# Crossbar transfers of one batch change places: each expert pair's first 512 tokens ahead of its last 64

## The chip, the cores and the metric

The kernel runs on one core of a Trainium2 chip. The metric is the device time of one execution in microseconds (us). An execution under the profiler gives a trace, and the profile is read from it. The core's engines are TensorE (PE in the profile, with its weight loads apart as PEld), VectorE (DVE), ScalarE (ACT), GpSimd (POOL) and SyncE (SP). They run their own instruction streams in order and wait for each other by semaphores. SyncE computes nothing here: it issues transfers, one after the other, and 16 DMA engines carry them out. A transfer is done when it has landed, some time after its issue.

## The reference

Two layers run one after the other. The first is attention of 8 heads over keys and values that are averaged over groups of 8 tokens:

```python
k_p = k.reshape(B, H, Sp, pool, D).mean(axis=3)
v_p = v.reshape(B, H, Sp, pool, D).mean(axis=3)
scores = scale * np.matmul(q, k_p.transpose(0, 1, 3, 2))
...
return np.matmul(attn, v_p).astype(np.float32)
```

The second takes its output as x (8 batches, 576 tokens, width 512) and runs four attention experts of width 64. Each token keeps two of the four by a gate:

```python
for e in range(E):
    q = x @ wq[e]
    k = x @ wk[e]
    v = x @ wv[e]
    scores = scale * (q @ k.transpose(0, 2, 1))
    causal = np.triu(np.ones((S, S), dtype=bool), 1)
    ...
    ye = a @ v @ wo[e]
    for kk in range(K):
        mask = topk[:, :, kk] == e
        out += mask[..., None] * w[:, :, kk:kk + 1] * ye
```

## The kernel before

The 8 batches go through the same stages, several batches under way at once. The order of the work is written out by hand as one long string of tokens, SEQ (L622 to L693). A loop (L696 to L748) turns each token into instructions, and each engine runs its own in the order in which they stand there. A token has a name, arguments, a batch and, where it uses PSUM, a bank: "Y1:5@6" is Y with tile 1 for batch 5 in bank 6. Capitals are mostly matmuls, and the same small letter the step that reads their result. A "d" behind a token puts its copy on VectorE rather than ScalarE, a "p" leaves the write to the output for a later token (zs).

The 576 tokens of a batch are four tiles of 128 and a last one of 64. Two batches share their buffers, and their two last tiles of 64 lie side by side as one tile of 128 (tile 4). The four experts are handled as two pairs: pair 0 and pair 1.

The steps around the change are these:

- P and p compute a batch's expert queries and keys and copy them to SBUF (tile qk). V and v do this for the values (vaug), along with the gate's logits. Steps g0 to g9 compute the gate.
- S computes expert scores into two PSUM banks, s (L493, ScalarE) takes their exponential into etb, and a (L510, GpSimd) sets the masked half of the diagonal blocks to zero.
- B (Bv) multiplies etb with the values. Then bz (L545), bg (L547) and b (L552) divide by the sums of the exponentials, apply the gate and write osc, one buffer of 128 partitions per pair and batch parity. For batches 2 to 5 a batch's B is cut in two parts. In an odd batch part 0 holds the shared tile 4 and the first two full tiles, part 1 the last two full tiles. So the main transfer needs both parts, and the tail transfer needs part 0.
- osc has tokens in partitions, and the output product needs the pair's 2 x 64 channels there. For batches 0, 1, 6 and 7 TensorE transposes it (T, t). For batches 2 to 5 a crossbar transfer does it: F, the function crossbar (L574). It is issued from SyncE's queue and goes from osc to oT. F00 is pair 0's first 512 tokens (L580, here called main 0), F01 pair 0's last 64 (L577, tail 0); F10 and F11 are main 1 and tail 1.
- Y (L582) multiplies a tile's columns of oT with wop: one matmul for pair 0, then one for pair 1, summed in one PSUM bank. y (L592) copies the result to ofin, a ring of nine buffers, and z (L607) writes it to the output: 256 KB a tile. zs1:2 is the write of batch 2's tile 1. These writes are issued by SyncE too, in one stream with the crossbar transfers.

For batch 5 the string has F01, zs1:2, F00, F11, zs0:2 and F10 in this order on SyncE. F01 stands after b01:5 and b00:5 on VectorE, F11 after b10:5 and b11:5. The first readers of the mains are Y1:5 and Y3:5, which are followed on TensorE by S03:6, S10:7 and S11:7. The first reader of the two tails is Y4:5 (L687 of the string), since tile 4 holds the last 64 tokens of batches 4 and 5. The framework puts in the waits: a matmul that reads oT waits for the semaphore of the very transfer that wrote those columns, and a transfer waits for the osc that it reads.

```python
if tail:
    nc.sync.dma_start(out=oT[:, tcols(b)], in_=own[half(b), 4 * (1 - b % 2), :], transpose=True)
else:
    c = b % 2
    nc.sync.dma_start(out=oT[:, mcols(b)].rearrange("p (c n) -> p c n", n=128), in_=own[:, c : c + 4, :].rearrange("p c n -> p (c n)"), transpose=True)
```

Of the kernel before, what the change touches and what calls it, by code (L numbers as in the profile page):

```python
# [21 lines left out]
def kernel(  # L22
# [584 lines left out]
    def z(b, c, queue):  # L607
# [69 lines left out]
        a02:5 p_t0:6d g0:6 S11:5@4 F01:4 S00:6@6 s12:5 g2:6 V3:7@3 g3:6 g4:6 B01:5@2 s00:6 v3:7d F00:4 a12:5 Y2:3@0  # L677
        bz01:5 V4:7@3 bg01:5 s11:5 b01:5 V2:7@1 a00:6 y2:3dp Y0:3@2 v2:7 S10:5@6 a11:5 zs2:3 v4:7 y0:3dp S12:6@4
        S01:6@0 s10:5 B00:5@3 g5:6 zs0:3 g6:6 g7:6 P_t0:7@2 s12:6 g8:6 a10:5 g9:6 P_q0:7@6 p_t0:7d s01:6 bz00:5 a12:6
        bg00:5 Y1:2@2 b00:5 V1:7@7 p_q0:7d y1:2p F01:5 a01:6 S10:6@0 v1:7 S11:6@4 zs1:2 S02:6@2 s10:6 B10:5@6 g1:7  # L680
        F00:5 g2:7 Y0:2@7 s02:6 bz10:5 a10:6 B11:5@0 bg10:5 b10:5 P_k0:7@1 s11:6 bz11:5 a02:6 bg11:5 b11:5 F11:5
        B00:6@6 y0:2dp Y3:4@2 p_k0:7 a11:6 Y1:4@0 bz00:6 y3:4p zs0:2 bg00:6 F10:5 B11:6@1 b00:6 y1:4p S02:7@4 zs3:4
        bz11:6 S01:7@2 g0:7 bg11:6 S00:7@6 zs1:4 s02:7 b11:6 P_q1:7@0 g3:7 g4:7 g5:7 s00:7 g6:7 B10:6@1 a02:7 T00:6@4
        P_k1:7@5 bz10:6 bg10:6 p_q1:7 t00:6d a00:7 b10:6 s01:7 T11:6@4 Y1:5@6 p_k1:7d Y3:5@7 t11:6d y1:5p S03:6@0 a01:7
        S10:7@2 y3:5dp S11:7@4 s03:6 zs1:5 Y2:5@6 s10:7 g7:7 a03:6 zs3:5 g8:7 T10:6@7 Y0:5@0 t10:6d y2:5p B01:6@1 g9:7
# [90 lines left out]
```

## Time and profile before

| | before |
|---|---|
| median of 3 runs | 156.94 us (156.93 to 157.01) |
| profiled execution | 157.23 us, span 155.5 us |
| TensorE busy | 145.2 us, 93% of the span |
| ScalarE busy | 137.8 us, 89% |
| VectorE busy | 124.2 us, 80% |
| GpSimd busy | 89.0 us, 57% |
| granted TensorE clock, mean | 0.994 |

All times inside the profile are counted in us from the start of the span. Busy time of an engine is no proof that it is the bound. That is read from the chain of work that ended last, which is followed back from the last instruction to what released each step. In the views by tile and by line "x8" is the number of instructions. In the instructions in order of time the columns are start, length, engine (SPq is SyncE's queue of issues), line, operation, output, input and count; the brackets at the end give the idle time of that engine just before and what ended it. The length of an SPq row is the time that SyncE spent on issuing, not the time until the transfer landed.

### The profile page before, as it was taken

Reading aid. Unit: us, or ns where it says so; the run is one execution under the profiler, and the core shown is the slowest. Engines: PE = TensorE matmul, PEld = TensorE weight load, DVE = VectorE, ACT = ScalarE, POOL = GpSimd, SP = SyncE. Lnnn points to the kernel's source line nnn. Section 1 sums busy time; section 2 is a strip of 40 time slices with the busy share of each in tenths; the row PEclk is TensorE's granted clock in tenths of the full one; section 3 lists DMA queues with packets and bytes.
Section 4 is the critical chain, followed back from the end, with each engine's and each line's share of the span. In section 5 each row is a group of like instructions: output and inputs, shape, how many; then the busy total and the mean of one; then the engine's idle time right before and its main releaser. Section 6 shows DMA issues by size and latency. Waiting matters only on the chain.

```text
span 155.5 us, 5467 instructions
## 1 busy us (share of the span) xinstructions
PE 145.2 (93%) x2131; PEld 79.1 (51%) x2131; DVE 124.2 (80%) x407; ACT 137.8 (89%) x255; POOL 89.0 (57%) x160
## 2 busy tenths in 40 slices
PE   6998998999999999999999999999999999969980
PEld 2332452454664365455736556475465765526640
DVE  1862826889889889989898999999988888957860
ACT  3369579999999999999999999999999999969970
POOL 6996488999689988855999141224100434323200
PEclk9999999999999999999999999999999999999997
DMA  4999999999999999999999963431480552387894
GB/s 121 239 187 184 177 179 180 180 180 190 180 179 180 182 177 181 213 251 178 180 180 213 181 75 76 146 104 34 126 279 8 108 173 72 82 198 267 282 377 161
DMA packets 68746, 26.67 MB, mean 171 GB/s; under 512 B 62704, under 2 KB 63728, under 8 KB 68720
## 3 DMA queue, kind: packets, MB, share of 16 engines
q0 software_dynamic: 57264, 14.72, 95.0%
q1 hardware_dynamic: 11088, 10.88, 22.8%
q10 hardware_dynamic: 368, 0.72, 1.5%
q8 instruction: 16, 0.26, 0.7%
q14 instruction: 10, 0.08, 0.2%
HBM read 30.42 MB, written 9.44 MB: 256 GB/s over the span
## 4 chain that ended last, share of the span: by engine, by line
PE 54%; DMA 19%; POOL 9%; ACT 7%; DVE 4%; issue 4%; POOLq 0%; SPq 0%; DVEq 0%; ACTq 0%
PE psum L220 53%; DMA qraw<-in_q_dram 11%; DMA wst_q<-in_moe_wq_dram 5%; DMA oT<-osc 3%; POOL kraw L125 3%; POOL qraw L125 3%; ACT eta L330 3%; ACT etb L493 2%; POOL vraw L125 1%; POOL etb L510 1%; PE psum L229 1%; DVE qT L297 1%; ACT rza L353 1%; ACT rza L349 1%; DVE osc L552 1%
## 5 line engine op out<-in xcount | busy, mean ns | idle before, releaser
L493 ACT ACTIVATE etb<-psum 128x1024 bf16<-128x1024 f32 x48 | 47.2, 1029 | 0.7 <-PE psum L220 0.4
L510 POOL TENSOR_SCALAR_AFFINE_SELECT etb<-etb 128x256 bf16<-128x256 bf16 x64 | 25.9, 416 | 30.0 <-ACT etb L493 29.1
L330 ACT ACTIVATE eta<-psum 96x1024 bf16<-96x1024 f32 (+1 forms) x48 | 36.0, 807 | 0.6 <-PE psum L220 0.2
L220 PEld LDWEIGHTS <-etb 128*128 128x128 bf16 x480 | 18.6, 97 | 7.9 <-issue 2.8
L376 DVE TENSOR_TENSOR xT<-psum,rza 128x512 bf16<-128x512 f32 x32 | 20.5, 681 | 2.1 <-ACT rza L353 2.0
L220 PE MATMUL psum<-wop,oT 128*128 128x512 bf16 (+1 forms) x74 | 20.4, 373 | 1.7 <-DMA oT<-osc 1.4
L125 POOL DMA_DIRECT2D qraw<-in_q_dram x29 | 19.1, 661 | 4.3 <-DMA vraw<-in_v_dram 2.9
L220 PE MATMUL psum<-vaug,etb 128*128 128x65 bf16 x480 | 21.2, 193 | 0.2 <-POOL etb L510 0.2
L125 POOL DMA_DIRECT2D kraw<-in_k_dram x25 | 19.0, 765 | 3.0 <-issue 0.9
L125 POOL DMA_DIRECT2D vraw<-in_v_dram x24 | 18.5, 774 | 3.7 <-PE psum L220 2.9
L220 PE MATMUL psum<-wvg,xT 128*128 128x260 bf16 x144 | 20.5, 274 | 0.0
L220 PE MATMUL psum<-xT,wqp 128*128 128x64 bf16 (+1 forms) x128 | 19.6, 286 | 0.0
L220 PE MATMUL psum<-xT,wkp 128*128 128x512 bf16 (+1 forms) x128 | 19.5, 286 | 0.0
L552 DVE TENSOR_TENSOR osc<-psum,gt 128x256 bf16<-128x256 f32 (+2 forms) x40 | 16.6, 422 | 1.0
L220 PE MATMUL psum<-qk 64*128 64x64 bf16 (+4 forms) x192 | 16.1, 277 | 0.2
L220 PEld LDWEIGHTS <-xT 128*128 128x128 bf16 x144 | 12.7, 97 | 6.3 <-issue 2.5
L211 ACT COPY ofin<-psum 128x512 f32<-128x512 f32 (+1 forms) x25 | 13.9, 581 | 2.1 <-PE psum L220 1.8
L211 DVE CAST qk<-psum 128x512 bf16<-128x512 f32 (+1 forms) x24 | 14.6, 615 | 1.3 <-PE psum L220 0.6
L297 DVE STREAM_TRANSPOSE qT<-qraw 128x576 f32<-128x576 f32 (+1 forms) x17 | 13.2, 789 | 2.9 <-DMA qraw<-in_q_dram 2.2
L220 PE MATMUL psum<-qT,kpT 32*128 32x64 bf16 (+1 forms) x256 | 13.3, 289 | 1.6 <-ACT eta L330 0.6
L208 PE MATMUL psum<-warm 128*128 128x512 bf16 x41 | 12.8, 461 | 1.3 <-DVE onesd L176 1.3
L220 PE MATMUL psum<-eta,vp 96*32 96x512 bf16 (+1 forms) x256 | 13.1, 288 | 0.2 <-DVE vp L211 0.2
(78 smaller groups left out, 215.8 us busy)
## 6 DMA issues: line engine op xcount, KB each, us to landing
out_dram<-ofin SPq DMA_DIRECT2D x32, 256.0 KB, 2.6
vraw<-in_v_dram POOLq DMA_DIRECT2D x24, 192.0 KB, 6.8
kraw<-in_k_dram POOLq DMA_DIRECT2D x21, 192.0 KB, 7.5
qraw<-in_q_dram POOLq DMA_DIRECT2D x28, 144.0 KB, 7.8
out_dram<-ofin SPq DMA_DIRECT2D x7, 128.0 KB, 2.5
xT<-in_q_dram ACTq DMA_DIRECT2D x2, 288.0 KB, 4.7
xT<-in_k_dram SPq DMA_DIRECT2D x2, 192.0 KB, 5.0
kraw<-in_k_dram POOLq DMA_DIRECT2D x4, 96.0 KB, 5.2
```

Of the source, the lines that this page charges most:

```text
L125: nc.gpsimd.dma_start(out=dst, in_=src)
L208: nc.tensor.matmul(out=psum[rows, bank, :], lhsT=warm[:, rows], rhs=warm[:], start=True, stop=True)
L211: (nc.vector.tensor_copy if dve else nc.scalar.copy)(out=out, in_=in_)
L220: nc.tensor.matmul(out=out, lhsT=lhsT, rhs=rhs, start=start, stop=stop)
L229: nc.tensor.transpose(out=out[s], in_=in_[:, s], identity=ident[0:n, 0:n])
L297: nc.vector.transpose(out=dst.rearrange("p (a s n) -> p a n s", s=32, n=n)[:, :, own], in_=src.rearrange("p (a n d) -> p a n d", n=n, d=32 ...
L330: nc.scalar.activation(out=dst, in_=src, func=EXP, scale=ATT_EXP_SCALE)
L349: nc.scalar.activation(out=rz, in_=z, func=LN)
L376: nc.vector.tensor_tensor(out=xT[:, 2 * got[0][0] + t : 2 * got[-1][0] + t + 1 : 2, m + got[0][1].start : m + got[0][1].stop], in0=psum[:, ...
L493: nc.scalar.activation(out=et[:, ep, :, eo : eo + n], in_=psum[:, bank : bank + 2, 0:n], func=EXP, scale=MOE_EXP_SCALE,)
L510: nc.gpsimd.affine_select(out=blk, in_=blk, pattern=[[0, 2], [1, 128]], compare_op=ISGE, fill=0.0, base=0, channel_multiplier=-1,)
L552: nc.vector.tensor_tensor(out=osc(b, ep)[:, own, :].rearrange("p c (e d) -> p e c d", e=2), in0=o[:, :, :, 0:HD], in1=gt.to_broadcast([128 ...
```

## The change

Four tokens of SEQ change places, all of batch 5: F01 with F00, and F11 with F10. After it each pair's first 512 tokens are issued before its last 64. Nothing else differs: the transfers themselves, their buffers and the instructions of TensorE, VectorE, ScalarE and GpSimd stay in the same order.

```diff
-        bg00:5 Y1:2@2 b00:5 V1:7@7 p_q0:7d y1:2p F01:5 a01:6 S10:6@0 v1:7 S11:6@4 zs1:2 S02:6@2 s10:6 B10:5@6 g1:7
-        F00:5 g2:7 Y0:2@7 s02:6 bz10:5 a10:6 B11:5@0 bg10:5 b10:5 P_k0:7@1 s11:6 bz11:5 a02:6 bg11:5 b11:5 F11:5
-        B00:6@6 y0:2dp Y3:4@2 p_k0:7 a11:6 Y1:4@0 bz00:6 y3:4p zs0:2 bg00:6 F10:5 B11:6@1 b00:6 y1:4p S02:7@4 zs3:4
+        bg00:5 Y1:2@2 b00:5 V1:7@7 p_q0:7d y1:2p F00:5 a01:6 S10:6@0 v1:7 S11:6@4 zs1:2 S02:6@2 s10:6 B10:5@6 g1:7
+        F01:5 g2:7 Y0:2@7 s02:6 bz10:5 a10:6 B11:5@0 bg10:5 b10:5 P_k0:7@1 s11:6 bz11:5 a02:6 bg11:5 b11:5 F10:5
+        B00:6@6 y0:2dp Y3:4@2 p_k0:7 a11:6 Y1:4@0 bz00:6 y3:4p zs0:2 bg00:6 F11:5 B11:6@1 b00:6 y1:4p S02:7@4 zs3:4
```

## The prediction

> **What bounds the kernel now.** I read the page's first part first, then the chain of work that ended last over the final 30 us, then the one transfer in it, then SyncE's own order.
>
> ```profile
> span 155.5 us, 5467 instructions
> PE 145.2 (93%) x2131; PEld 79.1 (51%) x2131; DVE 124.2 (80%) x407; ACT 137.8 (89%) x255; POOL 89.0 (57%) x160
> ```
>
> TensorE is busy for 93% of the span, so a gap in it counts. The chain, in order of time (start, length, what):
>
> ```profile
> 129.16 2.12 DMA oT<-osc
> 131.28 0.30 DVE osc L552
> ...
> 135.09 0.06 SPq L615
> ...
> 135.21 3.23 DMA oT<-osc
> 138.44 0.04 issue
> 138.48 1.96 PE psum L220 x15
> ...
> 150.53 0.62 PE psum L220 x4
> ```
>
> The chain leaves TensorE for a crossbar transfer issued at 135.21 and landing at 138.44, and goes on with TensorE's output matmuls at 138.48. The same transfer in the view of the tile oT, this one issue alone:
>
> ```profile
> L580 SPq DMA_TRANSPOSE oT<-osc x1: 1252/1252/1252, 135.2 to 135.2; - x1
> ...
> who waited for it (us, times):
>   PEld L220: 1.7, 1
>   PE psum L220: 1.4, 1
> ```
>
> L580 is the transfer of 512 tokens ("main"), L577 that of 64 tokens ("tail"). This is the last of batch 5's four, the main of expert pair 1 (token F10:5). The reader is to see that of 16 crossbar transfers the profile puts a TensorE wait on this one. The other transfer in the chain, at 129.16, is the tail of pair 0 (F01:5). I don't count it as a cost: that step leads to a VectorE instruction, and no wait of TensorE is put down to it. The stall itself, from the instructions in order of time (start, length, engine):
>
> ```profile
> 128.57 0.56 DVE L552 TENSOR_TENSOR osc<-psum,gt 128x384 bf16<-128x384 f32 x1
> ...
> 132.19 0.42 DVE L552 TENSOR_TENSOR osc<-psum,gt 128x256 bf16<-128x256 f32 x1
> ...
> 132.53 0.68 DVE L211 COPY ofin<-psum 128x512 f32<-128x512 f32 x1
> ...
> 136.56 1.05 ACT L493 ACTIVATE etb<-psum 128x1024 bf16<-128x1024 f32 x1
> ...
> 136.68 0.38 PE L220 MATMUL psum<-wop,oT 128*128 128x512 bf16 x1
> ...
> 138.48 0.82 PE L220 MATMUL psum<-wop,oT 128*128 128x512 bf16 x3 [1.42 <-DMA oT<-osc]
> 138.91 0.59 ACT L211 COPY ofin<-psum 128x512 f32<-128x512 f32 x1 [1.29 <-PE psum L220]
> 139.39 0.69 DVE L211 COPY ofin<-psum 128x512 f32<-128x512 f32 x1 [1.73 <-issue]
> ```
>
> Y1:5 multiplies the transposed outputs of both pairs with wo. Its matmul for pair 0 runs at 136.68, its matmul for pair 1 wants F10:5 and starts 1.42 us after TensorE came free at 137.06. ScalarE, out of work at 136.56 + 1.05 = 137.61, then waits 1.29 us for Y1:5's result, and VectorE stands 1.73 us. Three engines stand at once, so these us are on the path. Why F10:5 is late stands in SyncE's order:
>
> ```profile
> 129.16 1.10 SPq L577 DMA_TRANSPOSE oT<-osc  x1
> 130.35 0.54 SPq L615 DMA_DIRECT2D out_dram<-ofin  x1
> 130.94 2.32 SPq L580 DMA_TRANSPOSE oT<-osc  x1
> 133.35 1.18 SPq L577 DMA_TRANSPOSE oT<-osc  x1
> 134.62 0.53 SPq L615 DMA_DIRECT2D out_dram<-ofin  x1
> 135.21 1.25 SPq L580 DMA_TRANSPOSE oT<-osc  x1
> 136.55 7.95 SPq L615 DMA_DIRECT2D out_dram<-ofin  x8
> ```
>
> SyncE issues without a pause from 129.16 to 136.46: tail of pair 0, a write (zs1:2), main of pair 0, tail of pair 1, a write (zs0:2), main of pair 1. The data of F10:5 were ready when VectorE wrote osc (b11:5), at 132.19 + 0.42 = 132.61. It was issued 2.60 us later, because SyncE was busy with what stands ahead of it.
>
> **The change, part by part.** No instruction is added or removed. Within each pair, main and tail change places around one write; the issue order of the other four engines is the same. After it SyncE's order is main 0, zs1:2, tail 0, main 1, zs0:2, tail 1.
>
> *Main 0* takes the place of tail 0 at 129.16. Both wait for pair 0's last osc (b00:5, 128.57 + 0.56 = 129.13), so it starts no later; its first reader runs at 136.68.
>
> *Main 1* is the part that pays. What one issue costs, and how long it takes to land from its start (min/median/max; first the tails, then the mains):
>
> ```profile
> L577 SPq DMA_TRANSPOSE oT<-osc x8: 1103/1174/1727, 90.9 to 133.4; - x8
> ...
> DMA to landing us min/median/max: 2.3/2.4/4.1
> ```
>
> ```profile
> L580 SPq DMA_TRANSPOSE oT<-osc x8: 1240/1260/2316, 92.2 to 135.2; - x8
> ...
> DMA to landing us min/median/max: 2.5/2.6/4.5
> ```
>
> At median issues: main 0 to 129.16 + 1.26 = 130.42; zs1:2 0.09 later for 0.54, to 131.05; tail 0 0.05 later for 1.17, to 132.27. SyncE would then wait for b11:5, and main 1 starts at about 132.63. That is the early bound. The late one: in the rows of before one main's issue took 2.32 in place of 1.26. It ended at 133.26, when tail 0, with the longest landing of the tails (4.1 from 129.16), came in. About then there was an instruction fetch on the DMA engines; these are the DMA queues in 130.7 to 130.8, and in 136.4 to 136.5 (packets, MB, share of 16 engines):
>
> ```profile
> q8 instruction: 1, 0.02, 92.9%
> ```
>
> ```profile
> q14 instruction: 1, 0.01, 35.1%
> ```
>
> One packet of 0.929 x 16 x 0.1 = 1.49 us, thus until about 132.2 on one of the 16 engines. I take it as what held that issue (an inference from the times). If it now holds tail 0 until 133.26, main 1 starts 0.09 later, at 133.35, in place of 135.21. Landing: the median main takes 2.6, this one took 3.23 (with the second packet inside its time). So it lands between 132.63 + 2.6 = 135.2 and 133.35 + 3.23 = 136.6. Both ends are before 137.06, when TensorE wants it, by 0.5 us at least. At the longest landing of the rows, 4.5, it is 137.85, which is the end for the range. I take the inside: the median of the eight mains is 2.6, and the row of this very transfer, 3.23, is nearer to it than to the 4.5.
>
> [...]
>
> *Tail 0* moves from 129.16 to about 131.1, *tail 1* from 133.35 to behind zs0:2: main 1 ends its issue at 133.9 to 134.6, zs0:2 takes 0.53, and tail 1 starts at 134.5 to 135.2 and lands 2.3 to 4.1 later, by 139.3 at worst. Who waits for tails is Y4:5, whose second weight load in before is this one:
>
> ```profile
> 142.64 0.10 PEld L220 LDWEIGHTS <-oT 128*128 128x128 bf16 x1 [0.16 <-issue]
> ```
>
> 1.35 us earlier that is 141.3, 2.0 us after the worst landing. Cost nothing under that cover; without it, whatever tail 1 comes in late.
>
> *The two writes.* zs1:2 starts at 130.5 in place of 130.35, zs0:2 at 134.0 to 134.7 in place of 134.62; its data (copy at 132.53 + 0.68 = 133.21) are there. Their nine buffers come round nine copies later, at the last two copies of this row:
>
> ```profile
> 142.12 1.75 ACT L211 COPY ofin<-psum 128x512 f32<-128x512 f32 x3
> ```
>
> Even 1.35 us earlier, at 140.8, that is 6 us after zs0:2 starts, and no transfer of the rows above takes over 4.5 to land: nothing. Behind tail 1 SyncE is free at 135.7 to 136.4, in time for the write of 136.55.
>
> *The sum.* TensorE gains 1.42 at Y1:5. ScalarE can start Y1:5's copy only at 137.61, so it gains 138.91 - 137.61 = 1.30. VectorE's copy moves by the 1.42. Does the gain reach the end? By stages (busy us, count; then granted clock, DMA share, GB/s):
>
> ```profile
> 137.10:138.50 1.40, 0.02 (x1) 0.02 (x2) 0.56 (x2) 0.52 (x1) 0.41 (x1) 1.00 1.00 202
> 138.50:142.00 3.50, 3.50 (x46) 1.92 (x47) 2.22 (x8) 3.09 (x6) 0.85 (x2) 1.00 0.60 222
> ...
> 146.00:150.00 4.00, 4.00 (x53) 2.38 (x50) 3.27 (x13) 3.36 (x10) 0.42 (x1) 1.00 0.95 329
> 150.00:152.00 2.00, 0.86 (x6) 0.41 (x5) 0.81 (x3) 0.99 (x3) 0.00 (x0) 1.00 1.02 381
> ```
>
> From 138.5 on TensorE is full in the stages shown up to 150, at a clock of 1.00, and ScalarE nearly. Both move ahead together by 1.30 to 1.42; I take 1.35. The profiled execution took 157.23 us (span 155.5 and 1.73 around it); the median of the three runs is 156.94, 0.29 less. So span 154.15, profiled 155.9, median 156.94 - 1.35 = **155.6 us**.
>
> **The rivals.**
>
> *Part of the stall stays.* Main 1 starts at 133.35 but lands after 4.5 like the slowest main: 137.85 instead of 138.44. It gives back 0.59: 156.35. For it: a main did take 4.5, and this one took more than the median already. Against: the mains of 130.94 and 135.21 each had a write issued just ahead of them; in the new order tail 0 stands between zs1:2 and main 1.
>
> *The gain is taken by the next bound.* The writes fill the DMA engines from 146 on (shares 0.95 and 1.02). If they can't start earlier, the end stays: 156.9. Against: from 138.5 to 142 the share is 0.60, a free 0.40 x 3.5 = 1.4 us, just what the writes need to come forward.
>
> *Slower: SyncE is held more than once.* If main 0 and tail 0 are both held for 2.32, main 1 starts at 129.16 + 2.32 + 0.09 + 0.54 + 0.05 + 2.32 + 0.09 = 134.57, and with the longest landing comes at 139.07, 0.63 after the present 138.44: 157.57. It decides from 133.94 (138.44 - 4.5) on as the start of main 1. For it: main 0 is now the one in flight when the packet of 130.7 comes. Against: only one such packet lies in these us, and 1.49 us of it would have to make two holds of 1.06 and the long landing. [...]
>
> That the order at the engines doesn't change is excluded: SyncE issues in the order written.
>
> **How the numbers follow.** Chances: the forecast 0.68, part of the stall 0.11, next bound 0.07, slower 0.14. The likeliest alone is 155.3 (1.42 and some 0.2 for a shorter tail of writes) to 156.0. The range must take in the partial case: 155.3 to 156.6, which leaves out the last two, 0.21, rounded to 2 in 10. A change under 0.2% (0.31 us) can't be told from none. Faster 0.79 (the first two), same 0.07, slower 0.14.
>
> **What would show it.** Right: a main starts on SyncE at 129.16 and the next one between 132.6 and 133.4, landing before 137.06; no wait of TensorE on oT near Y1:5, its two matmuls back to back; Y1:5's copy on ScalarE near 137.6; TensorE's last four matmuls near 149.2 instead of 150.53. Wrong: a wait of TensorE on a DMA of oT at Y1:5 (part or slower, by its landing), at Y4:5 (tail 1), or writes with longer landings at an unmoved end.

## The result

| | before | after |
|---|---|---|
| median | 156.97 us (4 runs, 156.93 to 157.05) | 155.75 us (4 runs, 155.60 to 156.21) |
| profiled execution | 157.23 us, span 155.5 | 155.60 us, span 153.9 |

The ratio is 0.9924 with a 95% interval of 0.9900 to 0.9948, a gain of 1.22 us by the medians and 1.63 us between the two profiled executions. In a later series of runs, in which the kernel before took 157.22 us at the median, the changed kernel took 155.65 us (4 runs, 155.53 to 155.73): ratio 0.9904 (0.9878 to 0.9931). The forecast was 155.6. Medians count all runs, while the ratios leave out three slow ones, over 1.5% above the fastest of their kernel: one of 347.29 us of the kernel before, one of 158.91 and one of 159.76 of kernels below.

The chain of work that ended last, in the changed kernel from 120 on (start, length, what):

```profile
119.87 15.86 PE psum L220 x229
135.72 0.11 PE psum L229 x2
135.83 0.86 PE psum L220 x4
136.70 0.11 PE psum L229 x2
136.81 2.00 PE psum L220 x16
...
148.91 0.62 PE psum L220 x4
```

No crossbar transfer is left in it. It stays on TensorE through the place of the former stall, and the last four matmuls start at 148.91, where they started at 150.53 before: 1.62 earlier. SyncE's issues in the changed kernel:

```profile
129.12 1.21 SPq L580 DMA_TRANSPOSE oT<-osc  x1
130.42 0.53 SPq L615 DMA_DIRECT2D out_dram<-ofin  x1
131.00 2.21 SPq L577 DMA_TRANSPOSE oT<-osc  x1
133.30 1.22 SPq L580 DMA_TRANSPOSE oT<-osc  x1
134.61 0.53 SPq L615 DMA_DIRECT2D out_dram<-ofin  x1
135.19 1.12 SPq L577 DMA_TRANSPOSE oT<-osc  x1
```

Main 1 (the second L580 row) starts at 133.30 in place of 135.21. The long issue has gone from main 0 to tail 0 (2.21). The landing of main 1, from the DMA issues of its own moment:

```profile
oT<-osc SPq DMA_TRANSPOSE x1, 2.4
```

So main 1 is in at 135.7. The instructions around Y1:5, in order of time:

```profile
136.53 1.05 ACT L493 ACTIVATE etb<-psum 128x1024 bf16<-128x1024 f32 x1
...
136.65 1.03 PE L220 MATMUL psum<-wop,oT 128*128 128x512 bf16 x4
...
137.44 0.62 ACT L211 COPY ofin<-psum 128x512 f32<-128x512 f32 x1
...
137.76 0.69 DVE L211 COPY ofin<-psum 128x512 f32<-128x512 f32 x1
...
141.01 0.10 PEld L220 LDWEIGHTS <-oT 128*128 128x128 bf16 x1 [0.16 <-DMA out_dram<-ofin]
```

The four matmuls of Y1:5 and Y3:5 run back to back from 136.65. Y1:5's copy starts at 137.44 (138.91 before) and Y3:5's at 137.76 (139.39 before). The last row is Y4:5, the reader of the tails: its gap is 0.16, as it was before. Moving the tails back cost nothing. By stages (busy us, count; clock, DMA share, GB/s):

```profile
137.10:138.50 1.40, 1.40 (x15) 0.53 (x14) 1.26 (x4) 1.40 (x5) 0.47 (x2) 1.00 0.77 290
138.50:142.00 3.50, 3.50 (x54) 2.16 (x53) 2.90 (x14) 3.48 (x6) 1.16 (x3) 1.00 0.90 329
```

Where TensorE, VectorE and ScalarE stood, they work. The DMA share from 138.5 to 142 rose from 0.60 to 0.90: the writes came forward into the free time.

### The profile page after: what moved, and what is told of

It reads as the page before. It is cut to its first block, busy times and chain, and to the rows that moved or that the text cites. A ratio compares the mean times of both kernels' runs of the same rounds, so it can differ in the third digit from the quotient of the medians.

```text
span 153.9 us, 5467 instructions
## 1 busy us (share of the span) xinstructions
PE 143.7 (93%) x2131; PEld 78.9 (51%) x2131; DVE 125.2 (81%) x407; ACT 137.5 (89%) x255; POOL 88.9 (58%) x160
## 4 chain that ended last, share of the span: by engine, by line
PE 65%; DMA 9%; ACT 9%; POOL 8%; issue 3%; DVE 3%; SPq 0%; DVEq 0%; POOLq 0%
PE psum L220 62%; DMA qraw<-in_q_dram 6%; ACT eta L330 4%; DMA xT<-in_k_dram 4%; POOL qraw L125 3%; POOL kraw L125 2%; ACT etb L493 2%; PE psum L208 2%; POOL etb L510 2%; PE psum L229 1%; DVE qT L297 1%; ACT rza L353 1%; ACT rza L349 1%; POOL vraw L125 1%; DVE kf L277 1%
## 5 line engine op out<-in xcount | busy, mean ns | idle before, releaser
L353 ACT ACTIVATE rza<-rza 128x512 f32<-128x512 f32 (+1 forms) x24 | 12.6, 527 | 0.4
```

Of the source, the lines that this page charges most:

```text
L353: nc.scalar.activation(out=rz, in_=rz, func=EXP, scale=-1.0)
```

## The experiments

The theory at this point: the stall is the late landing of main 1 and nothing else. Its cause behind that, inferred in the prediction, is a fetch of instructions that holds one of SyncE's issues. The rivals: main before tail is better in itself, or the writes next to the transfers make them late. Ratios are against the kernel before in the same series; apart from the one of 347.29 its runs spread from 156.1 to 158.4 us, so the intervals reach some 0.3% to either side. What a trace shows, here and below, is one execution of each kernel.

**One pair at a time.** Only pair 1 changes places:

```diff
- ... bg11:5 b11:5 F11:5
+ ... bg11:5 b11:5 F10:5
- ... y3:4p zs0:2 bg00:6 F10:5 B11:6@1
+ ... y3:4p zs0:2 bg00:6 F11:5 B11:6@1
```

> Only pair 1's main and tail change places (F10:5 ahead of F11:5); pair 0 stays tail first. Theory (the gain is the earlier issue of main 1, and nothing else): tail 0 takes 129.16 as before, main 0's issue is held to about 133.3 by the instruction fetch, main 1 starts at about 133.35 and lands at about 135.8 to 136.6, so the stall of TensorE at Y1:5 is gone and the whole gain is there: 155.6 to 155.8. Rival (both swaps are needed, each brings about half): main 1 still comes in after 137.06 and the time is about 156.3.

155.80 us (6 runs), ratio 0.9903 (0.9868 to 0.9937), and no wait of TensorE on oT. The whole gain is in this half. Only pair 0:

```diff
- ... y1:2p F01:5 a01:6 ...
+ ... y1:2p F00:5 a01:6 ...
-        F00:5 g2:7 Y0:2@7
+        F01:5 g2:7 Y0:2@7
```

> Only pair 0's main and tail change places. Theory: main 1 stays last on SyncE and starts at about 135.2, the stall of 1.4 us at Y1:5 stays, time as before, 156.9 to 157.0. Rival (each swap brings about half): main 1's landing falls, the stall is about half, 156.3.

157.56 us (12 runs), ratio 1.0000 (0.9970 to 1.0031). The time is above the expected one, but the kernel before had 157.28 in this series. Main 1 stays last on SyncE and TensorE waits as before (SyncE's rows for zs1:2 and main 1, then TensorE's):

```profile
130.58 1.74 SPq L615 DMA_DIRECT2D out_dram<-ofin  x1
...
135.44 1.26 SPq L580 DMA_TRANSPOSE oT<-osc  x1
```

```profile
138.69 0.82 PE L220 MATMUL psum<-wop,oT 128*128 128x512 bf16 x3 [1.51 <-DMA oT<-osc]
```

The long issue fell on the write this time (1.74 in place of 0.54). One of the twelve runs took 155.72, the time of the changed kernel; it was not profiled, and what spared it stays open. The two results leave no room for "each brings half".

**Main 1 later or earlier by other means.** The kernel before, with main 1 one write further back:

```diff
- ... y3:4p zs0:2 bg00:6 F10:5 B11:6@1 b00:6 y1:4p S02:7@4 zs3:4
+ ... y3:4p zs0:2 bg00:6 B11:6@1 b00:6 y1:4p S02:7@4 zs3:4 F10:5
```

> The kernel before with main 1 moved one write further back, behind zs3:4. Theory (us for us: each us that main 1 lands later is a us at the end): main 1 starts 0.6 later, at about 135.8, lands at about 138.4 to 139.1, the stall grows from 1.4 to between 1.4 and 2.1, time 157.0 to 157.6, and the time above the kernel before is what the stall grew by. Rival (something else, such as the writes, takes up part of a stall): the stall grows and the time does not.

158.08 us (12 runs), ratio 1.0049 (1.0020 to 1.0078): slower by 0.5%, and above the expected range. In the profiled execution main 1 did not start 0.6 later but at 135.16, since main 0's issue was held for less this time (1.64); it landed 3.7 after its start, and TensorE waited 1.65, which is 0.23 more than before:

```profile
138.86 0.82 PE L220 MATMUL psum<-wop,oT 128*128 128x512 bf16 x3 [1.65 <-DMA oT<-osc]
```

Between the two profiled executions these matmuls start 0.38 later (138.86 against 138.48) and the span is 0.4 longer (155.9 against 155.5): us for us, as the theory has it. Why the medians lie further apart (158.08 against 157.28) is not shown.

The changed kernel, with main 1 behind zs0:2:

```diff
- ... bg11:5 b11:5 F10:5
+ ... bg11:5 b11:5
- ... y3:4p zs0:2 bg00:6 F11:5 B11:6@1
+ ... y3:4p zs0:2 F10:5 bg00:6 F11:5 B11:6@1
```

> The changed kernel with main 1 issued behind the write zs0:2 in place of ahead of it (tail 1 still last). Theory (there is slack between main 1's landing, 135.7, and 137.06, when TensorE wants it): main 1 starts at about 133.9, lands at 136.4 to 137.1 and the time is that of the changed kernel. Rival (any delay of main 1 counts): 0.6 us slower, 156.3.

155.73 us (7 runs), ratio 0.9919 (0.9889 to 0.9949). Main 1 started at 133.95, right behind a write, and landed 2.5 later, at 136.4, still in time. So a delay within the slack cost nothing at the median. Two of the seven runs took 156.34 and 156.59; whether main 1 was late in them no trace shows.

The tails left ahead, and the two writes moved behind main 1 instead:

```diff
- ... S11:6@4 zs1:2 S02:6@2 ...
+ ... S11:6@4 S02:6@2 ...
- ... y3:4p zs0:2 bg00:6 F10:5 B11:6@1
+ ... y3:4p bg00:6 F10:5 zs1:2 zs0:2 B11:6@1
```

> The kernel before with tails first as before, but the writes zs1:2 and zs0:2 moved behind main 1. Theory (anything that brings main 1 in before 137.06 gives the gain, not the order of mains and tails as such): main 1 starts at 134.0 to 134.6, lands at 136.5 to 137.8, the stall is 0 to 0.7 and the time 155.7 to 156.5. Rival (tails ahead of mains cost by themselves): the stall and the time stay as in the kernel before.

155.75 us (6 runs), ratio 0.9898 (0.9872 to 0.9925), the full gain with tails first. Main 0's issue was held for 1.63 only, so main 1 started earlier than expected. Main 1 on SyncE:

```profile
133.38 1.22 SPq L580 DMA_TRANSPOSE oT<-osc  x1
```

It is when main 1 comes in that counts, not the order of main and tail.

**Mains first in batch 4 as well.** Added to the changed kernel:

```diff
- F11:4 (line 674) ... F10:4 (676) ... F01:4 ... F00:4 (677)
+ F10:4 (line 674) ... F11:4 (676) ... F00:4 ... F01:4 (677)
```

> The changed kernel with batch 4's mains put ahead of its tails as well. Theory (a main's place matters only where TensorE waits for it; no TensorE wait on batch 4's transfers is in the profile): as the changed kernel, within 0.2%. Rival (mains first is better in itself, since it takes load off the queue earlier): another gain, 0.3 us or more.

155.88 us (6 runs), ratio 0.9905 (0.9874 to 0.9937). This kernel left a part of the computation out: at line 674 only one of the two parts of main 1's data is written, so it moved old values for the rest. The same idea with each main where its data are complete:

```diff
- F11:4 (line 674) ... F10:4 (676) ... F01:4 ... F00:4 (677)
+                      F10:4 F11:4 (676) ... F00:4 ... F01:4 (677)
```

> The changed kernel with batch 4's tails put behind their mains too, each main where its data are complete (in the earlier run of this idea main 1 of batch 4 went out before the first half of its data was written, so it moved old values there). Theory (a main's place matters only where TensorE waits for it): the time of the changed kernel within 0.2%. Rival: a further gain of 0.3 us or more.

155.57 us (6 runs, 155.40 to 155.67), ratio 0.9882 (0.9857 to 0.9907). The changed kernel itself had 155.65 and 0.9904 in its own comparison; the difference of 0.08 us is inside 0.2%. Nothing waits for these transfers, and their order is worth nothing that these runs can tell.

**The changed kernel again,** for its spread:

> The changed kernel once more, for its spread. Theory: 155.6 to 155.8 in most runs. If main 1 sometimes comes in late, single runs lie at up to 156.4; if not, the run of 156.21 was of the loads early in the kernel, and runs stay under 156.0.

155.65 us, 155.53 to 155.73. No run near 156.2 came back; the cause of that one run stays open.

**The fetch.** Some of the warm-up matmuls at the start of the kernel make room for tiny ones, so that TensorE has 128 more instructions and all that follows lies later in its program. The order of the transfers is that of before:

```diff
+def filler(n, bank):
+    for _ in range(n):
+        nc.tensor.matmul(out=psum[0:32, bank, 0:32], lhsT=warm[0:KR, 0:32], rhs=warm[0:KR, 0:32], start=True, stop=True)
...
- H14:0@0 L_k20:0
+ H6:0@0 G72:0@0 L_k20:0
```

> The kernel before with 128 more instructions on TensorE at the very start (8 of the 14 first warm-up matmuls are left out and 72 tiny ones put in their place; the order of the transfers is that of before). Theory (the issue of main 0 took 2.32 us because a block of TensorE's instructions was fetched at 130.7): the block comes about 4 us earlier in the work, near 126.5, main 0's issue takes 1.26 us, tail 1 and main 1 move forward by about 1 us, main 1 lands at about 136.7 to 137.3 and nearly all of the stall is gone without any change of the order: 155.6 to 156.1. Rival (the write issued just ahead holds the transfer, or the fetch is another engine's): main 0's issue takes 2.3 us as before and the time is 156.9.

157.93 us (12 runs), ratio 1.0047 (1.0022 to 1.0073). The first half of the expectation held and the second missed. SyncE's rows (line numbers are 4 higher here), main 0 and then main 1:

```profile
131.02 1.25 SPq L584 DMA_TRANSPOSE oT<-osc  x1
...
134.22 1.71 SPq L584 DMA_TRANSPOSE oT<-osc  x1
```

The fetch of 130.7 now comes at 125.4. Main 0's issue is back to 1.25, and main 1 starts 1.0 earlier. But the next fetch now comes at 134.5, into main 1's own flight, and so does one of the smaller packets of q14. The DMA queues in 134.5 to 134.6 and in 136.4 to 136.5, main 1's landing, and TensorE's wait:

```profile
q8 instruction: 1, 0.02, 60.0%
```

```profile
q14 instruction: 1, 0.01, 47.8%
```

```profile
oT<-osc SPq DMA_TRANSPOSE x1, 4.1
```

```profile
138.41 0.82 PE L224 MATMUL psum<-wop,oT 128*128 128x512 bf16 x3 [1.27 <-DMA oT<-osc]
```

Landing after 4.1 rather than 3.2 ate nearly the whole us that was won. The page of this kernel counts 17 packets on that queue, against 16 in the kernel before, and still 10 on q14:

```profile
q8 instruction: 17, 0.28, 0.7%
q14 instruction: 10, 0.08, 0.2%
```

The instructions that were added are all TensorE's, so q8 is TensorE's queue. The same filler in the changed kernel:

> The changed kernel with the same 128 more instructions on TensorE. Theory: tail 0's issue takes about 1.2 us in place of 2.2, main 1 starts at 132.6, as soon as its data are there; the stall was gone already, so the time is that of the changed kernel, 155.6 to 155.8. Rival (the fetch costs time also where it holds nothing that TensorE waits for, or the filler costs): faster or slower than the changed kernel by over 0.3 us.

156.13 us (11 runs), ratio 0.9943 (0.9919 to 0.9967). Tail 0's issue took 1.13 and main 1 started at 132.68, both as expected. With a fetch at 134.7 in its flight main 1 landed after 4.1, at 136.8, and TensorE did not wait: the slack covered it. It was close: the four matmuls started at 136.73, and the second of them, which reads main 1, some 0.2 later. The time is still 0.3% to 0.4% above the changed kernel.

With half the filler (10 warm-ups, 36 tiny matmuls, 64 more instructions) the fetches should miss both mains:

```diff
- H14:0@0 L_k20:0
+ H10:0@0 G36:0@0 L_k20:0
```

> The kernel before with 64 more instructions on TensorE at the start (4 of the 14 first warm-ups left out, 36 tiny ones in their place). With 128 more, the fetch of TensorE's instructions that used to come at 130.7 came at 125 and the next one at 134.5, in main 1's own flight. With 64 more they should come near 128 and 138 to 139, so that none lies in the flight of main 0 or main 1. Theory (fetches made main 0's issue long, and whether main 1 is late hangs on them): main 0's issue takes 1.25, main 1 starts at about 134.2 and lands 2.5 to 3.2 later, at 136.7 to 137.4; the stall is under 0.4 us and the time about 156.0, with the order of before. Rival (main 1 is late for its place alone): it lands after 138 as in all runs in which it is last, and the time stays at that of the kernel before.

156.37 us (7 runs), ratio 0.9943 (0.9911 to 0.9975), with the order of before. The DMA queues in 127.4 to 127.5, which is ahead of all four transfers (the next one came at 138.0):

```profile
q8 instruction: 1, 0.02, 102.6%
```

SyncE's rows, in the old order:

```profile
129.03 1.11 SPq L581 DMA_TRANSPOSE oT<-osc  x1
130.23 0.54 SPq L619 DMA_DIRECT2D out_dram<-ofin  x1
130.82 1.25 SPq L584 DMA_TRANSPOSE oT<-osc  x1
132.17 1.18 SPq L581 DMA_TRANSPOSE oT<-osc  x1
133.44 0.53 SPq L619 DMA_DIRECT2D out_dram<-ofin  x1
134.02 1.26 SPq L584 DMA_TRANSPOSE oT<-osc  x1
```

TensorE's Y1:5 and Y3:5:

```profile
136.56 1.03 PE L224 MATMUL psum<-wop,oT 128*128 128x512 bf16 x4
```

Main 1 started at 134.02, landed 2.5 later, at 136.5, and the stall is gone: the four matmuls run as in the changed kernel. This profiled execution was the fastest of the seven (155.88). The control:

> The changed kernel with the same 64 more instructions, as a control on what they cost by themselves. Theory: no stall as before, time that of the changed kernel plus what the filler costs; with 128 more it was 0.4% above the changed kernel, so 0.1 to 0.4% here. Rival: the filler is free, and the 0.4% came from a fetch in the flight of a transfer; then 155.7.

156.30 us (7 runs), ratio 0.9927 (0.9899 to 0.9955). With the fetch out of the way the new order and the old one are alike (156.30 and 156.37). So the stall of the kernel before took both: the order that put main 1 last, and TensorE's fetch falling into the transfers ahead of it.

All the traces can be counted for this. The 14 of them hold 224 crossbar transfers, 16 each. For 87 of these no instruction packet of q8 or q14 ran on the DMA engines between the start of the issue and the landing: their issues took 1.10 to 1.27 and they landed after 2.20 to 2.66. Every longer issue (up to 2.71) and every longer landing (up to 4.77) had such a packet in its time. The reverse does not hold: a packet that ended soon after the issue began, or came just before the landing, often did no harm. q14's packets are shorter (0.3 to 1.0 us), but where one of them alone began 1.1 to 2.1 after the start of a transfer, this landed after 2.8 to 3.7. Main 1 of the kernel before is one of these: its 3.23 had q14's packet of 136.5 in it. With half the filler q14's packet came at 136.3, when main 1 had run for 2.3, and the landing stayed at 2.5. So of the 1.4 us of stall some 0.7 came by q14's packet (an estimate, 3.23 less 2.5), which met main 1 because main 1 was late already.

What the filler costs, 0.2% to 0.4% by ratios and medians, lies at the end. It brings a 17th fetch, at 145 to 148, among the last writes. In the ten traces with 16 fetches the last write landed 2.7 after the end of the last compute instruction. In the four with 17 it took 3.0, 3.1, 3.2 and, in this control, 3.9. Up to there the work is hardly later: the first of the four transfers starts at 129.0 to 129.4 with the filler and without, although with 128 more instructions the granted clock was 0.90 to 0.96 over the first 30 us, where the kernel before has 1.00. The landings of the last two writes, first of the changed kernel, then with half the filler in the old order, then in this control:

```profile
out_dram<-ofin SPq DMA_DIRECT2D x1, 128.0 KB, 2.3
out_dram<-ofin ACTq DMA_DIRECT2D x1, 128.0 KB, 2.6
```

```profile
out_dram<-ofin SPq DMA_DIRECT2D x1, 128.0 KB, 2.7
out_dram<-ofin ACTq DMA_DIRECT2D x1, 128.0 KB, 3.0
```

```profile
out_dram<-ofin ACTq DMA_DIRECT2D x1, 128.0 KB, 3.5
out_dram<-ofin SPq DMA_DIRECT2D x1, 128.0 KB, 3.6
```

The control's profiled execution was the slowest of its seven (157.07), so its 3.9 is not the usual cost.

## Why the prediction was right, point by point

*Main 0 takes tail 0's place at 129.16.* It did, at 129.12. TensorE's fetch, 0.5 later than before (131.2), fell into its flight and it landed after 4.1, still over 3 us ahead of its reader. *Main 1 pays.* The late bound was the true one: tail 0 held until 133.26 and main 1 at 133.35 by the working, 133.21 and 133.30 by the trace. *The landing* was 2.4, just under the near end of 2.6 to 3.23: q14's packet of 136.4 came at 136.6 in the changed kernel, when main 1 was in already (135.7).

*The inference that the fetch held the issue* was the weakest step, and the runs bear it out: with the fetch moved away main 0's issue is 1.25 in place of 2.32, and none of the 87 transfers without a packet has an issue over 1.27.

*The tails and the two writes at nothing.* Right: Y4:5's gap stayed at 0.16.

*The sum* was a little small inside the trace: 1.35 forecast, 1.62 at the last matmuls. The term that was mis-sized is the 1.42. It is the idle time between the end of one matmul row and the start of the next, but consecutive matmuls overlap: four of them take 1.03, while a single one has a length of 0.38. The second would have started about 0.2 before the first one ended, so the stall was 1.6 from start to start, and TensorE wanted main 1 at 136.9 rather than 137.06. ScalarE was no bound either: its copy began at 137.44, 0.14 before the end of the row ahead of it, not at 137.61. Against the medians the forecast gain of 1.35 is 0.13 too large in the first series (1.22) and 0.22 too small in the later one (1.57); that it lies between them is in part luck.

*The rivals.* The next bound did not take the gain; the writes came forward. "Part of the stall stays" did not happen, but its premise, a main 1 that lands after 4 us, is real: in the changed kernel with 128 more instructions it landed after 4.1, and only an early start (132.68) saved it. The argument against this rival, that the long mains had a write issued just ahead of them, pointed at the wrong thing: main 1 right behind zs0:2 landed after 2.5. Against "SyncE is held more than once" the prediction had that one packet would not make two holds and the long landing. No trace shows one packet lengthening the issues of two transfers, but the rest was too strong: in the changed kernel, with one packet of 0.95 us in the time of both (131.2), main 0 landed after 4.1, and tail 0's issue (2.21) and landing (3.3) were long as well. It did not come to a slower kernel because main 1 was behind all of that and still in by 135.7, 1.1 us before TensorE wanted it.

## What to carry to other kernels

When TensorE waits on a transfer, look at what the issuing queue did from the moment its data were ready; put the one transfer that is waited for ahead of those that are not, and leave the rest alone. Give it slack, up to 2 us where it can be had, because landings took that much longer here with an unrelated instruction fetch in their time (4.8 at most, against 2.2 to 2.7 without). When an issue or a landing is long once and short elsewhere, look for an instruction packet in the DMA queues at that moment before blaming the neighbours.

## What the runs showed that was not expected

With a fetch of TensorE's instructions (one packet of 0.02 MB that took 0.9 to 1.8 us) in their time, crossbar transfers landed after as much as 4.8 us, against 2.2 to 2.7 without one, and one of SyncE's issues behind them took as much as 2.7, against 1.1 to 1.3. With the smaller packets of q14 alone landings went up to 3.7. Sixty-four more instructions at the very start, over 120 us earlier, were enough to move the fetch off (127.4 in place of 130.7) and remove the same stall; of the 1.0% that the new order wins 0.6% is left, since the filler costs 0.2% to 0.4%. How one packet of about a us goes with a delay of up to 2 us of a whole transfer was not taken apart. Nor was a version tried that has the new order and one fetch fewer, which these runs suggest as the next step.
